# New order lists for a three-engine attention and gated-MLP kernel, with LayerNorm statistics on VectorE in some blocks and the last output transfers moved

## The chip, the cores and the metric

One NeuronCore of one Trainium2 chip runs the whole kernel. The metric is device time in microseconds (us), the median of several executions. One further execution was recorded by the hardware profiler, and the durations below come from it.

Engine names in the profile: PE is TensorE (PEld its weight loads), DVE is VectorE, ACT is ScalarE, POOL is GpSimd, SP is SyncE, which here issues nearly all DMA transfers. A trailing q (SPq) marks the sequencer of an engine.

## The reference

Eight batches, eight heads, 576 positions, head dimension 64. Attention keeps only the scores within `tau` of the row's maximum; a gated MLP with a spatial projection follows.

```python
scores = scale * q @ k^T                                # 64 problems of 576 x 576
scores = where(scores >= max(scores) - tau, scores, -1e9)
attn   = exp(scores - max) ; attn /= sum(attn)
x      = (attn @ v), heads side by side                 # [8, 576, 512]
h      = relu(x @ w_in) ; u, v = h[:512], h[512:]
v_n    = (v - mean(v)) / sqrt(var(v) + 1e-6)            # over the 512 features
v_s    = w_spatial @ v_n + b_spatial                    # over the 576 positions
out    = (u * v_s) @ w_out
```

## The kernel before

**Pairs and steps.** Heads are worked in pairs, four pairs to a batch. A pair has four row blocks of 128 positions; the last 64 positions of two pairs share one block more. So a batch has 18 steps, and step `g` is one block of 128 rows by 2 heads by 576 columns of scores. The scores lie in a ring of two PSUM tiles (`s_ring`), so step g+2 can begin on TensorE only when step g's scores have been read.

**A step in tokens.** `S` computes most of the scores on TensorE (line 678), `G` is an empty instruction on POOL that waits for the first of them, `Y` computes the rest behind `G` (they share a bank), `M` takes the negated maxima on VectorE (line 708). Then there are two ways:
- on the ScalarE path (`on_act`, listed in `ON_ACT`), `B` turns the maxima into biases (line 714), `E` and `F` apply a Prelu with a huge negative slope to the two heads (line 723), so that scores under the threshold become hugely negative, and `Z` takes the exponentials of both heads at once (line 743);
- on the VectorE path, `E` and `F` are exponentials (line 726), and `W` masks them with one VectorE instruction (line 738).

Two blocks of numerators are then turned by a DMA transpose on SyncE: `T` (`turn_p`, line 749), and `TR` for the shared block (line 755). Some of these are done on TensorE instead (`RP`).

**Around the steps.** `QA`/`QB`/`QR` transpose q and k on TensorE, and `qa`/`qb`/`qr` evict them; `kd` and `sq`/`sv` are POOL's copies. `P` and `p` multiply with v and divide (lines 376 to 390), likewise `R`/`r`. `XP`/`xp` and `X` transpose the result x, on TensorE or by DMA. The MLP of the batch before runs between the steps: `v` (lines 514 to 529), `u` (576), `s` (605) and `o` (634) are matmul groups, and `ev`, `eu`, `es`, `eo` their evictions. `L` issues loads, `C..` prepares the weights (`Ci` is w_in, `Cs` the spatial matrix, `Co` w_out, `Cb` the bias), `OUT1` and `OUT3` send two finished output blocks each (line 653), and `OUT4` the last 64 rows (line 566). A leading `d` puts an eviction on VectorE instead of ScalarE.

**LayerNorm in a block.** The evictions of `v` take five instructions over three engines: `ev` is a Relu on ScalarE with the row sums (line 537, followed by a read of the accumulator), `n` makes the negated mean on POOL (line 545), `k` squares on ScalarE with a sum (line 551, again with a read), and `N` makes the reciprocal root and the normalised block with four POOL instructions (lines 557 to 561).

**The order.** The order is written out. `ORDER` holds four lists of tokens; batch 0 runs the first, batch 1 the second, batch 2 the third, and batches 3 to 7 all run the fourth. A token `s1:2` means "for the batch two before this one", `L1:-1` "for the next". Each engine works its own instructions in the order in which the tokens issue them, and semaphores do the rest; nothing is reordered at run time. After the lists come the two tokens of `LAST` (the last mask and the last transpose), and then a tail without lists: the rest of batch 6's MLP and the whole of batch 7's, whose LayerNorm uses `bn_stats` and `bn_aggr` on VectorE (lines 784 and 786).

Of the kernel before, what the change touches and what calls it, by code (L numbers as in the profile page):

```python
# [16 lines left out]
    "L1:-1 L7:0 S0:0 G0:0 Y0:0 L0:-1 S1:0 M0:0 G1:0 Y1:0 QA1:0 L8:0 M1:0 E0:0 QR1:0 F0:0 B1:0 qa1:0 W0:0 "  # L17
    "S2:0 E1:0 G2:0 Y2:0 F1:0 dqr1:0 M2:0 Z1:0 S3:0 G3:0 kd1:0 Y3:0 E2:0 T00:0 QB1:0 M3:0 F2:0 qb1:0 B3:0 "
    "W2:0 F3:0 S4:0 E3:0 G4:0 Y4:0 Z3:0 M4:0 S5:0 Ci1:0 G5:0 Y5:0 sq2:0 L4:-1 QR2:0 B4:0 M5:0 Ci2:0 F4:0 "
    "QB2:0 E4:0 Cb0:0 dqb2:0 Z4:0 S6:0 T01:0 dqr2:0 B5:0 G6:0 sv0:0 Y6:0 F5:0 RP01:0 M6:0 QA2:0 E5:0 "  # L20
    "rp01:0 B6:0 qa2:0 QR3:0 E6:0 S7:0 G7:0 F6:0 Y7:0 M7:0 Z5:0 Ci0:0 S8:0 G8:0 kd2:0 L9:0 Y8:0 sq3:0 "
    "Z6:0 B7:0 M8:0 sv1:0 qr3:0 QB3:0 E7:0 RP00:0 B8:0 F7:0 kd3:0 T10:0 Cis1:0 drp00:0 E8:0 S9:0 F8:0 "
    "G9:0 Y9:0 Z8:0 M9:0 S10:0 G10:0 sq0:-1 Y10:0 Z7:0 B9:0 dqb3:0 Cis0:0 Cs1:0 M10:0 F9:0 QA3:0 L6:-1 "
    "R0:0 E9:0 dqa3:0 S11:0 B10:0 r0:0 G11:0 Cbs0:0 F10:0 Y11:0 P00:0 E10:0 M11:0 T11:0 sv2:0 Z9:0 S12:0 "
    "G12:0 sv3:0 B11:0 Y12:0 F11:0 P10:0 M12:0 Cis2:0 E11:0 Z11:0 Ci3:0 p00:0 L3:-1 p10:0 P01:0 Z10:0 "
    "Cs2:0 S13:0 p01:0 G13:0 sq1:-1 B12:0 Y13:0 F12:0 M13:0 T20:0 P11:0 E12:0 Css2:0 XP0:0 p11:0 dxp0:0 "
    "XP1:0 B13:0 E13:0 dxp1:0 QA0:-1 S14:0 F13:0 L2:-1 G14:0 Cis3:0 qa0:-1 Y14:0 L5:-1 QR0:-1 M14:0 "
    "QB0:-1 qr0:-1 Css4:0 XR0:0 Z12:0 S15:0 dqb0:-1 G15:0 F14:0 kd0:-1 Y15:0 P20:0 M15:0 E14:0 T21:0 "
    "Z13:0 S16:0 G16:0 B15:0 Css3:0 p20:0 Y16:0 E15:0 M16:0 F15:0 L7:-1 S17:0 W14:0 F16:0 G17:0 L8:-1 "
    "Y17:0 Z15:0 M17:0 E16:0 W16:0 T30:0 P21:0 F17:0 E17:0 p21:0 L9:-1 Cs0:0 "),  # L30
(
    "RP11:1 S0:0 G0:0 Y0:0 drp11:1 WS2:1 M0:0 RP10:1 ws2:1 S1:0 rp10:1 G1:0 Y1:0 B0:0 E0:0 QR1:0 M1:0 "
    "QA1:0 qr1:0 F0:0 qa1:0 B1:0 S2:0 W17:1 E1:0 G2:0 sq2:0 Y2:0 F1:0 QB1:0 M2:0 T31:1 Z0:0 XP2:1 S3:0 "
    "G3:0 sv1:0 qb1:0 dxp2:1 Y3:0 F2:0 M3:0 P30:1 kd1:0 E2:0 QB2:0 Z1:0 S4:0 B3:0 p30:1 G4:0 Y4:0 Co0:1 "
    "E3:0 QA2:0 M4:0 Css0:1 L5:-1 F3:0 qa2:0 S5:0 dqb2:0 Z3:0 G5:0 Y5:0 B4:0 W2:0 QR2:0 T00:0 P31:1 qr2:0 "
    "E4:0 R1:1 p31:1 F4:0 M5:0 XP3:1 S6:0 xp3:1 G6:0 kd2:0 Y6:0 r1:1 E5:0 L1:-1 M6:0 F5:0 WS0:1 L4:-1 "
    "v0:1 Z4:0 B6:0 S7:0 dws0:1 ev0:1 W5:0 G7:0 sq3:0 Y7:0 F6:0 T01:0 v1:1 E6:0 M7:0 RP00:0 ev1:1 S8:0 "
    "Z6:0 G8:0 n0:1 drp00:0 Cos0:1 Y8:0 QB3:0 M8:0 sv0:0 E7:0 L0:-1 v2:1 qb3:0 Css1:1 XR1:1 F7:0 QA3:0 "
    "E8:0 W7:0 S9:0 n1:1 ev2:1 G9:0 Y9:0 F8:0 T10:0 v3:1 dqa3:0 sv3:0 M9:0 S10:0 ev3:1 G10:0 k0:1 Y10:0 "
    "B9:0 P01:0 M10:0 E9:0 N0:1 u3:1 Co1:1 F9:0 B10:0 L3:-1 p01:0 S11:0 eu3:1 L6:-1 W8:0 G11:0 E10:0 "  # L40
    "Y11:0 F10:0 QR3:0 v4:1 dqr3:0 M11:0 Z10:0 T11:0 u1:1 ev4:1 S12:0 deu1:1 F11:0 G12:0 kd3:0 Y12:0 "
    "sq0:-1 Z9:0 RP01:0 P00:0 drp01:0 n2:1 L8:-1 M12:0 n3:1 u0:1 E11:0 n4:1 Cos1:1 k2:1 S13:0 B12:0 eu0:1 "
    "p00:0 G13:0 N2:1 Y13:0 F12:0 QB0:-1 M13:0 k1:1 T20:0 P11:0 qb0:-1 sq1:-1 p11:0 E12:0 WS4:1 B13:0 "
    "R0:0 dws4:1 Z12:0 sv2:0 QR0:-1 r0:0 S14:0 E13:0 L2:-1 G14:0 dqr0:-1 N1:1 W11:0 Y14:0 F13:0 QA0:-1 "
    "k4:1 WS3:1 M14:0 S15:0 k3:1 qa0:-1 G15:0 Y15:0 T21:0 B14:0 dws3:1 WS1:1 N3:1 F14:0 dws1:1 u4:1 E14:0 "
    "M15:0 P20:0 Z13:0 S16:0 B15:0 G16:0 eu4:1 p20:0 kd0:-1 Y16:0 N4:1 E15:0 Co2:1 XP0:0 M16:0 P10:0 "
    "F15:0 L7:-1 Z15:0 TR1:0 S17:0 dxp0:0 G17:0 p10:0 Y17:0 E16:0 M17:0 P21:0 F16:0 s0:1 Z14:0 p21:0 "
    "W16:0 u2:1 E17:0 T30:0 Cos2:1 eu2:1 es0:1 F17:0 Co3:1 XR0:0 L9:-1 "),
(
    "S0:0 G0:0 Y0:0 XP2:1 M0:0 QR1:0 S1:0 qr1:0 xp2:1 G1:0 kd1:0 Y1:0 sq2:0 B0:0 E0:0 QB1:0 M1:0 QA1:0 "  # L50
    "F0:0 qb1:0 S2:0 B1:0 W17:1 E1:0 G2:0 Y2:0 qa1:0 s1:2 F1:0 M2:0 T31:1 Z0:0 XP1:1 S3:0 B2:0 es1:2 G3:0 "
    "F2:0 sv0:0 Y3:0 dxp1:1 s2:2 E2:0 M3:0 sq3:0 Z1:0 QB2:0 L0:-1 B3:0 es2:2 S4:0 F3:0 L7:-1 G4:0 E3:0 "
    "Y4:0 L5:-1 P30:1 M4:0 qb2:0 Z2:0 S5:0 G5:0 p30:1 T00:0 Y5:0 B4:0 QR2:0 M5:0 s3:2 E4:0 qr2:0 F4:0 "
    "QA2:0 es3:2 F5:0 S6:0 dqa2:0 Z4:0 G6:0 Cos3:2 Y6:0 sv1:0 P31:1 M6:0 E5:0 R1:1 kd2:0 Z3:0 TR0:0 p31:1 "
    "S7:0 G7:0 r1:1 sv2:0 Y7:0 F6:0 o0:2 M7:0 X1:1 E6:0 o1:2 eo0:2 W6:0 T01:0 F7:0 o2:2 E7:0 W5:0 S8:0 "
    "eo1:2 G8:0 eo2:2 Y8:0 o3:2 M8:0 L4:-1 v0:1 eo3:2 L1:-1 B8:0 W7:0 E8:0 S9:0 ev0:1 G9:0 Y9:0 F8:0 u2:1 "
    "M9:0 T10:0 Z8:0 QR3:0 S10:0 deu2:1 G10:0 n0:1 F9:0 sv3:0 Y10:0 dqr3:0 v1:1 M10:0 E9:0 QA3:0 ev1:1 "
    "OUT3:2 W9:0 S11:0 qa3:0 G11:0 sq0:-1 E10:0 Y11:0 v2:1 M11:0 F10:0 k0:1 s4:2 kd3:0 W10:0 ev2:1 T11:0 "
    "S12:0 G12:0 F11:0 n2:1 Y12:0 es4:2 E11:0 QB3:0 M12:0 v3:1 qb3:0 u1:1 W11:0 ev3:1 L9:-1 F12:0 n3:1 "
    "S13:0 L3:-1 E12:0 G13:0 N0:1 Y13:0 eu1:1 u3:1 M13:0 k2:1 P00:0 k3:1 T20:0 B13:0 S14:0 p00:0 eu3:1 "  # L60
    "G14:0 N3:1 W12:0 F13:0 Y14:0 v4:1 E13:0 M14:0 R0:0 ev4:1 L2:-1 S15:0 r0:0 F14:0 G15:0 OUT4:2 n1:1 "
    "N2:1 Y15:0 k1:1 QB0:-1 M15:0 OUT1:2 P01:0 qb0:-1 E14:0 p01:0 T21:0 P20:0 N1:1 B15:0 P10:0 E15:0 "
    "p20:0 F15:0 S16:0 p10:0 G16:0 n4:1 W14:0 Y16:0 k4:1 QR0:-1 u4:1 qr0:-1 kd0:-1 QA0:-1 M16:0 eu4:1 "
    "N4:1 u0:1 qa0:-1 L8:-1 Z13:0 P11:0 B16:0 L6:-1 deu0:1 S17:0 p11:0 F16:0 G17:0 sq1:-1 Y17:0 Z15:0 "
    "s0:1 M17:0 E16:0 T30:0 P21:0 es0:1 F17:0 p21:0 E17:0 Z16:0 TR1:0 X0:0 "),
(
    "S0:0 G0:0 Y0:0 QA1:0 M0:0 QR1:0 qa1:0 S1:0 qr1:0 G1:0 B0:0 Y1:0 W17:1 E0:0 QB1:0 F0:0 s1:2 M1:0 "
    "qb1:0 Z0:0 S2:0 T31:1 G2:0 es1:2 Y2:0 B1:0 s3:2 M2:0 F1:0 E1:0 R1:1 sv1:0 es3:2 S3:0 B2:0 r1:1 F2:0 "
    "L3:-1 G3:0 kd1:0 Y3:0 sq2:0 E2:0 L1:-1 s2:2 M3:0 Z1:0 sq3:0 S4:0 B3:0 es2:2 F3:0 G4:0 Y4:0 T00:0 "
    "E3:0 o0:2 M4:0 Z2:0 P30:1 deo0:2 S5:0 B4:0 p30:1 G5:0 E4:0 Y5:0 F4:0 QA2:0 M5:0 L0:-1 P31:1 Z3:0 "  # L70
    "S6:0 p31:1 qa2:0 G6:0 sv2:0 Y6:0 X1:1 F5:0 o1:2 M6:0 sv3:0 E5:0 o2:2 eo1:2 W5:0 T01:0 E6:0 QB2:0 "
    "F6:0 S7:0 eo2:2 G7:0 W6:0 Y7:0 qb2:0 S8:0 Z4:0 G8:0 sv0:0 Y8:0 M7:0 L7:-1 QR2:0 s4:2 qr2:0 L4:-1 "
    "kd2:0 v0:1 es4:2 E7:0 M8:0 v1:1 F7:0 ev0:1 W7:0 S9:0 T10:0 ev1:1 G9:0 Y9:0 F8:0 n1:1 QR3:0 o3:2 "
    "dqr3:0 M9:0 E8:0 v2:1 k1:1 W8:0 eo3:2 S10:0 L6:-1 ev2:1 G10:0 n0:1 TR0:0 Y10:0 E9:0 P01:0 n2:1 M10:0 "
    "kd3:0 sq0:-1 F9:0 P00:0 k0:1 S11:0 B10:0 p01:0 F10:0 T11:0 G11:0 N0:1 p00:0 Y11:0 E10:0 QB3:0 M11:0 "
    "v3:1 qb3:0 Z10:0 W9:0 QA3:0 S12:0 OUT3:2 ev3:1 G12:0 dqa3:0 Y12:0 E11:0 OUT1:2 v4:1 M12:0 F11:0 u1:1 "
    "ev4:1 W11:0 T20:0 S13:0 eu1:1 n4:1 G13:0 Y13:0 B12:0 N1:1 E12:0 QR0:-1 M13:0 R0:0 qr0:-1 F12:0 "
    "QA0:-1 k2:1 S14:0 B13:0 r0:0 G14:0 F13:0 N2:1 Y14:0 dqa0:-1 E13:0 P10:0 L8:-1 M14:0 Z12:0 P11:0 "
    "OUT4:2 n3:1 L2:-1 S15:0 p10:0 k4:1 G15:0 kd0:-1 p11:0 Y15:0 F14:0 N4:1 u4:1 M15:0 T21:0 P20:0 eu4:1 "
    "E14:0 u0:1 p20:0 k3:1 B15:0 W14:0 u2:1 F15:0 E15:0 S16:0 deu0:1 Z13:0 G16:0 N3:1 Y16:0 deu2:1 u3:1 "  # L80
    "M16:0 Z15:0 X0:0 QB0:-1 sq1:-1 S17:0 eu3:1 B16:0 dqb0:-1 G17:0 E16:0 TR1:0 Y17:0 s0:1 F16:0 M17:0 "
    "Z16:0 T30:0 P21:0 es0:1 E17:0 p21:0 F17:0 L5:-1 L9:-1 ")]
LAST = "W17:1 T31:1"
ON_ACT = [(1, 3, 4, 5, 6, 7, 8, 9, 10, 11, 12, 13, 15), (0, 1, 3, 4, 6, 9, 10, 12, 13, 14, 15), (0, 1, 2, 3, 4, 8, 13, 15, 16), (0, 1, 2, 3, 4, 10, 12, 13, 15, 16)]


@with_exitstack
def kernel(
    ctx: ExitStack,
    tc: tile.TileContext,  # L90
    q: bass.AP,
    k: bass.AP,
# [427 lines left out]
    def moe_v(b, c):  # L520
# [13 lines left out]
        def ev():  # L534
# [4 lines left out]
            if c == 4 and b:  # L539
                o = hold["o"] = orr.tile([P, 512], F32, name="o")  # L540
                nc.scalar.copy(out=o[64:128], in_=hold["t"][64:128])
# [503 lines left out]
```

## Time and profile before

| what | us |
|---|---|
| median of 8 executions | 446.6 |
| lowest, highest | 445.94, 447.68 |
| the profiled execution's own time | 446.49 |
| its span, first to last instruction | 444.6 |
| busy: PE, DVE, ACT, POOL | 413.5, 394.0, 388.1, 181.4 |

The granted TensorE clock was 0.998 over the span. The span is the time from the first instruction to the last; 1.9 us of that execution's own time lie outside it. A row of a group gives the line, engine, operation, tiles and shapes, the count, then the busy time and the mean of one in ns, and then the idle time of the engine just before these instructions with what ended it. A row of the chain of waits gives start, length and what ran or was waited for. A row of the busy time by stretch gives the stretch, its length, the busy time and number of instructions of each engine, the clock, the DMA share and GB/s.

Two instructions of one engine can overlap by about a tenth of a microsecond, so the mean duration is longer than what one instruction adds to its engine's queue. TensorE's busy time includes matmuls in flight and says less about how much room it has.

### The profile page before, as it was taken

What the parts mean: (1) busy time and instruction counts of PE and PEld (TensorE: products, weight loads), DVE (VectorE), ACT (ScalarE), POOL (GpSimd) and SP (SyncE); (2) the same over time, 40 slices, a digit from 0 to 9 for tenths busy, and PEclk for the clock granted to TensorE, in tenths of its full rate; (3) what the DMA queues carried; (4) which work ended last, traced back from release to release, by engine and by line L of the source; (5) the groups of instructions that cost most, each with busy time, mean ns of one, the idle gap of its engine ahead of it and who ended that gap; (6) DMA issues with size and microseconds to landing.
All of it is one profiled execution on the core that took longest, in us unless ns stands there. A gap on an engine that the chain in (4) does not pass through costs nothing.

```text
span 444.6 us, 12872 instructions
## 1 busy us (share of the span) xinstructions
PE 413.5 (93%) x5035; PEld 259.6 (58%) x5035; DVE 394.0 (89%) x615; ACT 388.1 (87%) x649; POOL 181.4 (41%) x403
## 2 busy tenths in 40 slices
PE   7776789989999899999999999999999999999995
PEld 4445565565656666665565666566665666566542
DVE  5878889899899889999999999999999999999673
ACT  3997999999989899999899998999899998999351
POOL 1255334573215724354343533455343523354031
PEclk9999999999999999999999999999999999999999
DMA  7999999799999999999999999999999997998713
GB/s 189 283 260 201 247 229 193 138 213 205 215 174 243 193 199 198 191 229 218 200 206 203 251 174 206 238 206 234 192 215 196 250 188 148 162 210 122 169 35 108
DMA packets 222556, 88.15 MB, mean 198 GB/s; under 512 B 193568, under 2 KB 218272, under 8 KB 222496
## 3 DMA queue, kind: packets, MB, share of 16 engines
q1 hardware_dynamic: 221840, 86.45, 95.2%
q8 instruction: 40, 0.66, 0.6%
q0 software_dynamic: 160, 0.52, 0.3%
q10 hardware_dynamic: 496, 0.36, 0.2%
q14 instruction: 20, 0.16, 0.1%
HBM read 32.79 MB, written 9.44 MB: 95 GB/s over the span
## 4 chain that ended last, share of the span: by engine, by line
PE 32%; DVE 24%; ACT 18%; issue 7%; DMA 4%; POOL 2%; DVEq 0%; POOLq 0%; SPq 0%; ACTq 0%
PE s L678 13%; DVE p L738 7%; ACT e L726 7%; DVE s L708 6%; DVE negm L708 5%; PE f L605 4%; ACT e L723 4%; PE f L576 3%; PE f L329 3%; PE f L381 2%; ACT p L743 2%; DVE xn L390 2%; DMA ptr<-pr 2%; ACT vrel L537 2%; ACT sq L551 1%
## 5 line engine op out<-in xcount | busy, mean ns | idle before, releaser
L678 PE MATMUL s<-qkT 64*64 64x160 f32 (+1 forms) x2304 | 172.3, 415 | 11.0 <-ACT e L723 6.4
L678 PEld LDWEIGHTS s<-qkT 64*64 64x64 f32 x2304 | 106.7, 131 | 66.2 <-ACT e L723 15.7
L723 ACT ACTIVATE e<-s,negm 128x576 f32<-128x576 f32 x166 | 115.1, 743 | 14.7 <-DVE negm L714 6.3
L708 DVE TENSOR_REDUCE s<-s 128x2 f32<-128x1152 f32 x83 | 113.1, 1362 | 13.0 <-PE s L678 10.6
L726 ACT ACTIVATE e<-s,negm 128x576 f32<-128x576 f32 x122 | 85.6, 753 | 7.7 <-DVE negm L708 7.3
L708 DVE TENSOR_REDUCE negm<-s 128x2 f32<-128x1152 f32 x61 | 82.4, 1351 | 8.8 <-PE s L678 6.8
L738 DVE SCALAR_TENSOR_TENSOR p<-e,ctau 128x1152 bf16<-128x1152 f32 x61 | 86.3, 1417 | 3.3 <-ACT e L726 3.2
L743 ACT ACTIVATE p<-e 128x1152 bf16<-128x1152 f32 x67 | 78.2, 1172 | 0.4
L215 POOL CAST v<-vl 128x512 bf16<-128x512 f32 x32 | 21.0, 658 | 72.6 <-PE s L678 68.4
L381 PE MATMUL f<-v,pT 128*128 128x65 bf16 x1008 | 44.6, 194 | 0.0
L381 PEld LDWEIGHTS <-pT 128*128 128x128 bf16 x1024 | 41.5, 98 | 2.3 <-issue 0.4
L545 POOL TENSOR_SCALAR nmean<-sm 128x1 f32<-128x1 f32 (+1 forms) x35 | 15.8, 458 | 55.0 <-PE s L678 34.5
L390 DVE TENSOR_TENSOR xn<-f,r 128x256 bf16<-128x256 f32 (+1 forms) x93 | 35.4, 381 | 2.9
L605 PE MATMUL f<-wsT,vn 128*128 128x512 bf16 x135 | 33.6, 380 | 0.0
L576 PE MATMUL f<-xT,w_in 128*128 128x512 bf16 x120 | 30.8, 380 | 0.8 <-DVE negm L714 0.4
L376 PE MATMUL f<-v,pT 128*128 128x130 bf16 x126 | 27.8, 220 | 2.3 <-DVE r L388 1.5
L192 POOL COPY qn<-ql 128x512 f32<-128x512 f32 x31 | 20.1, 647 | 21.1 <-PE s L678 20.2
L561 POOL TENSOR_SCALAR vn<-vrel,rs,nm 128x512 bf16<-128x512 f32 (+1 forms) x35 | 26.8, 767 | 3.8
L529 PE MATMUL f<-w_in,xT 128*128 128x512 bf16 x112 | 27.9, 379 | 0.2 <-ACT vrel L537 0.2
L551 ACT ACTIVATE sq<-vrel,nmean 128x512 bf16<-128x512 f32 (+1 forms) x35 | 25.8, 736 | 1.7 <-POOL nmean L545 1.5
L634 PE MATMUL f<-w_o,gT 128*128 128x512 bf16 x100 | 24.6, 379 | 1.2 <-ACT qkT L309 1.2
L341 POOL COPY qkT<-qkT 64x64 f32<-64x64 f32 x32 | 7.5, 235 | 39.8 <-PE s L678 19.8
(159 smaller groups left out, 588.4 us busy)
## 6 DMA issues: line engine op xcount, KB each, us to landing
vl<-in_v_dram SPq DMA_DIRECT2D x16, 512.0 KB, 5.1
kl<-in_k_dram SPq DMA_DIRECT2D x15, 512.0 KB, 4.9
ql<-in_q_dram SPq DMA_DIRECT2D x15, 512.0 KB, 4.8
out_dram<-oo SPq DMA_DIRECT2D x12, 512.0 KB, 4.2
uT<-in_moe_w_in_dram SPq DMA_DIRECT2D x3, 512.0 KB, 5.1
uT<-in_moe_w_spatial_dram SPq DMA_DIRECT2D x2, 576.0 KB, 5.3
vx<-in_v_dram SPq DMA_DIRECT2D x16, 64.0 KB, 3.5
pT<-p SPq DMA_TRANSPOSE x64, 6.1
```

The source lines that it names most:

```text
L381: nc.tensor.matmul(out=t[:, at + 65 * h:at + 65 * h + 65], lhsT=pt[:, 5 * h + j, :], rhs=vt[:, 6 * h + j, :], start=False, stop=(h == 1 an ...
L390: nc.vector.tensor_tensor(out=dst, in0=o[ps, g0:g1, 0:64], in1=r[ps, g0:g1].unsqueeze(2).broadcast_to([ps.stop - ps.start, g1 - g0, 64]), ...
L529: nc.tensor.matmul(out=t, lhsT=x_of(b, f, slice(c * P, (c + 1) * P)), rhs=w_in[:, f, 512:1024], start=(f == 0), stop=(f == 3))
L551: nc.scalar.activation(out=sq[:n], in_=hold["vrel"][:n], func=ACT.Square, bias=hold["nmean"][:n], accum_out=ss[:n])
L576: nc.tensor.matmul(out=t, lhsT=w_in[:, m, f * P:(f + 1) * P], rhs=x_of(b, m, slice(0, 512)), start=(m == 0), stop=(m == 3))
L605: nc.tensor.matmul(out=t, lhsT=vn[:, c, f * P:(f + 1) * P], rhs=wsT[:, c, 0:512], start=(c == 0), stop=(c == 4))
L678: made.append(nc.tensor.matmul(out=s_ring[g % 2][halves[k], at[h] + lo:at[h] + hi], lhsT=qks[n][halves[h], 0, m:m + 64], rhs=qks[n][halves ...
L708: nc.vector.tensor_reduce(out=nm, in_=view(s_ring[g % 2], at[0], [[at[1] - at[0], 2], [1, S]]), axis=AX.X, op=ALU.max, negate=True)
L723: nc.scalar.activation(out=e, in_=s, func=ACT.Prelu, bias=bias_, scale=scale if steps[g][1] == 4 else 1.0, alpha=1e30)
L726: nc.scalar.activation(out=e, in_=s, func=ACT.Exp, bias=bias_)
L738: nc.vector.scalar_tensor_tensor(out=numerators(g), in0=ef, scalar=ctau, in1=ef, op0=ALU.is_ge, op1=ALU.mult)
L743: nc.scalar.activation(out=numerators(g), in_=e_ring[g % 3].rearrange("p h s -> p (h s)"), func=ACT.Exp)
```

## The change

1. All four lists are written anew. The order of scores, maxima, exponentials, evictions, loads and MLP groups differs throughout; the fourth list stays closest to what it was.
2. In some blocks the LayerNorm statistics go to VectorE: token `bv` is the Relu without sums, `bs` is `bn_stats` and `bn_aggr`, and `n` and `k` fall away. `N` keeps its four POOL instructions.
3. `ON_ACT` changes in the first three lists: from 13, 11, 9 and 10 steps to 11, 11, 12 and 10.
4. `M` can be split into one maximum for each head, tokens `H` and `K` (steps 4 and 17 of the second list, step 11 of the third).
5. `OUT` tokens of the last batch (7) are held and run after `LAST`, that is, behind the last transposed transfer on SyncE. In the fourth list `OUT1` and `OUT3` also move from the middle to the end.

```diff
-ON_ACT = [(1, 3, 4, 5, 6, 7, 8, 9, 10, 11, 12, 13, 15), (0, 1, 3, 4, 6, 9, 10, 12, 13, 14, 15), (0, 1, 2, 3, 4, 8, 13, 15, 16), (0, 1, 2, 3, 4, 10, 12, 13, 15, 16)]
+ON_ACT = [(1, 3, 4, 5, 7, 8, 10, 11, 12, 13, 15), (0, 2, 3, 4, 6, 9, 11, 12, 13, 15, 16), (0, 1, 3, 4, 5, 6, 9, 11, 12, 13, 14, 16), (0, 1, 2, 3, 4, 10, 12, 13, 15, 16)]
...
-        def ev():
+        def ev(sums=True):
             vrel = hold["vrel"] = vr.tile([P, 512], F32, name="vrel")
-            sm = hold["sm"] = small.tile([P, 1], F32, name="sm")
-            nc.scalar.activation(out=vrel[:n], in_=hold["t"][:n], func=ACT.Relu,
-                                 accum_out=sm[:n])
+            if sums:
+                sm = hold["sm"] = small.tile([P, 1], F32, name="sm")
+                nc.scalar.activation(out=vrel[:n], in_=hold["t"][:n], func=ACT.Relu,
+                                     accum_out=sm[:n])
+            else:
+                nc.scalar.activation(out=vrel[:n], in_=hold["t"][:n], func=ACT.Relu)
...
+        def stats():
+            st = small.tile([P, 6], F32, name="st")
+            mv = hold["mv"] = small.tile([P, 2], F32, name="mv")
+            nc.vector.bn_stats(out=st[:n], in_=hold["vrel"][:n])
+            nc.vector.bn_aggr(out=mv[:n], in_=st[:n])
...
-            nc.gpsimd.tensor_scalar(out=rs[:n], in0=hold["ss"][:n], scalar1=1.0 / 512,
-                                    scalar2=1e-6, op0=ALU.mult, op1=ALU.add)
+            if "mv" in hold:
+                nc.gpsimd.tensor_scalar(out=rs[:n], in0=hold["mv"][:n, 1:2], scalar1=1.0,
+                                        scalar2=1e-6, op0=ALU.mult, op1=ALU.add)
+            else:
+                nc.gpsimd.tensor_scalar(out=rs[:n], in0=hold["ss"][:n], scalar1=1.0 / 512,
+                                        scalar2=1e-6, op0=ALU.mult, op1=ALU.add)
...
-    def top(g):
+    def top(g, heads=slice(0, 2)):
...
+        elif kind == "OUT" and it == B - 1 and (name, b) not in held:
+            held.append((name, b))
+            return
...
         for tok in LAST.split():
             run_token(tok, B)
+        for name, b in held:
+            run_token(name, b)
```

The end of the fourth list, before and after:

```diff
-    "OUT4:2 n3:1 L2:-1 S15:0 p10:0 k4:1 G15:0 kd0:-1 p11:0 Y15:0 F14:0 N4:1 u4:1 M15:0 T21:0 P20:0 eu4:1 "
-    "E14:0 u0:1 p20:0 k3:1 B15:0 W14:0 u2:1 F15:0 E15:0 S16:0 deu0:1 Z13:0 G16:0 N3:1 Y16:0 deu2:1 u3:1 "
-    "M16:0 Z15:0 X0:0 QB0:-1 sq1:-1 S17:0 eu3:1 B16:0 dqb0:-1 G17:0 E16:0 TR1:0 Y17:0 s0:1 F16:0 M17:0 "
-    "Z16:0 T30:0 P21:0 es0:1 E17:0 p21:0 F17:0 L5:-1 L9:-1 ")]
+    "S14:0 qa0:-1 G14:0 B13:0 N2:1 bs4:1 Y14:0 F13:0 P10:0 L9:-1 M14:0 E13:0 P11:0 L2:-1 Z12:0 OUT4:2 "
+    "S15:0 p10:0 G15:0 N4:1 E14:0 Y15:0 p11:0 u4:1 M15:0 T21:0 P20:0 eu4:1 F14:0 u0:1 B15:0 k3:1 p20:0 "
+    "S16:0 deu0:1 E15:0 G16:0 N3:1 Y16:0 F15:0 u2:1 M16:0 Z13:0 u3:1 deu2:1 kd0:-1 Z15:0 TR1:0 sq1:-1 "
+    "S17:0 B16:0 deu3:1 G17:0 E16:0 Y17:0 W14:0 F16:0 QB0:-1 X0:0 s0:1 qb0:-1 M17:0 Z16:0 P21:0 T30:0 "
+    "es0:1 F17:0 p21:0 E17:0 OUT1:2 OUT3:2 ")]
```

Blocks whose statistics move, by list: none in the first; blocks 0, 2, 3, 4 in the second; all five in the third; blocks 1 and 4 in the fourth. Evictions marked `d` in each list: 9, 14, 5, 7 before and 4, 11, 4, 6 after.

## The prediction

> **What bounds the kernel now.** I first read the page's busy shares and the engine shares of the chain that ended last.
>
> ```profile
> PE 413.5 (93%) x5035; PEld 259.6 (58%) x5035; DVE 394.0 (89%) x615; ACT 388.1 (87%) x649; POOL 181.4 (41%) x403
> ...
> PE 32%; DVE 24%; ACT 18%; issue 7%; DMA 4%; POOL 2%; DVEq 0%; POOLq 0%; SPq 0%; ACTq 0%
> ```
>
> No engine owns the time: three are near 90% and the chain changes hands among them. So the second view is busy time by stretch. I cut where each batch's first score matmul starts (rows two to nine are batches 0 to 7; before them is the start-up, after them the tail).
>
> ```profile
> core 0: us, PE busy (x) PEld busy (x) DVE busy (x) ACT busy (x) POOL busy (x), PEclk, DMA share, GB/s
> 0.00:7.40 7.40, 5.08 (x23) 3.71 (x23) 3.43 (x20) 2.97 (x5) 0.92 (x7) 1.00 0.68 181
> 7.40:54.00 46.60, 34.31 (x475) 23.09 (x475) 37.13 (x57) 39.48 (x54) 20.60 (x44) 1.00 1.08 241
> 54.00:106.20 52.20, 47.19 (x612) 30.75 (x612) 47.78 (x75) 49.07 (x82) 26.68 (x56) 1.00 0.97 202
> 106.20:159.30 53.10, 50.88 (x629) 32.32 (x628) 48.10 (x68) 47.73 (x84) 23.02 (x50) 1.00 1.00 204
> 159.30:210.20 50.90, 50.06 (x622) 31.33 (x620) 48.01 (x71) 48.56 (x83) 20.59 (x49) 1.00 1.07 207
> ...
> 311.20:361.60 50.40, 49.91 (x623) 31.41 (x620) 47.70 (x71) 47.44 (x82) 21.81 (x49) 1.00 1.03 212
> 361.60:409.50 47.90, 46.88 (x586) 29.14 (x584) 44.91 (x67) 44.98 (x79) 19.30 (x44) 1.00 0.86 158
> 409.50:444.60 35.10, 29.50 (x261) 15.15 (x257) 21.80 (x51) 13.59 (x23) 4.70 (x6) 0.97 0.42 110
> ```
>
> The reader is to see that batches 3 to 6, which all run the fourth list, take 50.3 to 50.9 us with VectorE idle for only 2.7 to 3.2 us. Batches 1 and 2 take 52.2 and 53.1 with VectorE idle 4.4 and 5.0. Batch 0 has 9.5 idle. There is room in the first three lists and little in the fourth. The clock is full, so the clock explains nothing.
>
> Third, the groups with their shapes apart give the price of what the change touches.
>
> ```profile
> L551 ACT ACTIVATE sq<-vrel,nmean 128x512 bf16<-128x512 f32 x28 | 20.7, 740 | 0.1
> L537 ACT ACTIVATION_READ_ACCUMULATOR vrel<-f 128x1 f32 x28 | 6.2, 221 | 0.0
> L551 ACT ACTIVATION_READ_ACCUMULATOR sq<-vrel,nmean 128x1 f32 x28 | 6.1, 217 | 0.0
> L545 POOL TENSOR_SCALAR nmean<-sm 128x1 f32<-128x1 f32 x28 | 8.4, 309 | 37.8 <-PE s L678 34.5 <-ACT vrel L537 3.4
> L784 DVE BATCH_NORM_STATS2 st<-vrel 128x6 f32<-128x512 f32 x4 | 2.7, 686 | 0.7 <-ACT vrel L782 0.7
> L786 DVE BATCH_NORM_AGGREGATE mv<-st 128x2 f32<-128x6 f32 x4 | 0.7, 182 | 0.1
> ```
>
> The last batch already takes its statistics on VectorE (L784, L786), so the added operation has a row. Last, the SyncE queue and the chain at the end of batch 7:
>
> ```profile
> 398.50 0.55 SPq L566 DMA_DIRECT2D out_dram<-o  x1
> ...
> 409.50 7.92 SPq L749 DMA_TRANSPOSE pT<-p  x2
> 417.58 0.47 SPq L649 DMA_DIRECT2D out_dram<-ql  x1
> ...
> 411.98 1.27 ACT e L726 x2
> 413.27 1.42 DVE p L738
> 414.69 1.81 DVE gT L619 x3
> 416.54 0.39 PE t L634
> ```
>
> Batch 7 ends on ScalarE (an almost unbroken run of its instructions from 398 us), then one mask and three gates on VectorE, and only then the output products.
>
> **Statistics.** A block whose token becomes `bv`/`bs` loses the square, two accumulator reads and POOL's mean. What ScalarE gets back is start to start, not the sum of durations, since neighbours overlap: in the timeline a square starts at 399.38 and the instruction behind its read at 400.09 (0.71); the Relu's read costs 0.10 (read 394.64, next start 394.74). That is 0.81 per block. VectorE pays the pair: statistics start at 423.12, the instruction behind the aggregate at 424.06, so 0.94, more than 686+182 ns because the aggregate waits for its own input. Counting tokens: none in batch 0, 4 blocks in batch 1, 5 in batch 2, 2 in each of 3 to 7: 19 blocks.
>
> **Steps moved between engines.** A step on the ScalarE path costs ScalarE 1172+2x743 ns and VectorE 1366+155; on the other path 2x753 and 1351+1417. Moving one costs VectorE 1.25 us or gives it back. `ON_ACT` has 13, 11, 9, 10 steps before and 11, 11, 12, 10 after.
>
> **Evictions.** A `d` token puts an eviction on VectorE (0.68 for 512 columns of f32, 0.29 for 128, 0.41 for `xp`, about 0.45 for `rp`). The tokens go from 9, 14, 5, 7 to 4, 11, 4, 6.
>
> **VectorE by batch.** 0: two more masks, +2.5, against evictions -2.5: zero. 1: statistics +3.7, evictions -1.0, split maxima +0.2: +2.9. 2: statistics +4.7, three masks fewer -3.75, evictions -0.4, one split maximum +0.1: +0.6. 3 to 6: statistics +1.9, `qa0` and `qb0` back to ScalarE -1.4, `eu3` +0.7: +1.2 each. 7: the same without `qa0` and `qb0`, which it never had: +2.5. Sum +10.8. ScalarE gets about 2.4, 0.2, 0.9 (four times) and 2.2 back in batches 1 to 7: 8.4. TensorE's work is unchanged; POOL loses 19 means of 0.3 to 1.0 us.
>
> **Where I weigh a rule.** VectorE is busy 47.7 of 50.4 us in a fourth-list batch, ScalarE 47.4. The Trainium skill (Perfetto Trace Analysis, Identifying the Most-Contended Engine) says that for these two engines occupancy is a fair measure of the limit and that the most occupied one is to be relieved first; this change loads it. Carried one to one to the end, +10.8 makes 457.4. But the rows show batch 2 at 53.1 us and batch 5 at 50.3 with VectorE busy 48.1 and 47.6: order is worth more here than half a microsecond of occupancy. I take the rows: new length = VectorE's new busy time + the idle time that is left.
>
> **The idle time left.** In a fourth-list batch the 2.7 idle us contain 1.4 of waiting for scores and 0.5 for other named waits. The scores are late because ScalarE frees the score bank late (weight loads wait 1.0 and 0.6 us on its two forms of `e`). ScalarE now has 0.9 us less to do, so I take 1.0 off: 1.7. Between no relief (2.7) and no wait at all (about 0.8) that is my choice, and the ends go into the range.
> - Batches 3 to 6: 48.8+1.7 = 50.5 against 50.9, 50.7, 50.3, 50.4: -0.3 in all.
> - Batch 1: 50.7+1.7 = 52.4: +0.2.
> - Batch 2: 48.7+2.3 = 51.0: -2.1. More idle time is left since TensorE is busy 50.9 there.
> - Batch 0: equal load, 9.5 idle. 3.4 of it is one ramp wait that stays; two reorderable waits of 1.5 (the `xp` evictions at 43.6 to 46 us) should halve: -0.8.
> - Batch 7: 47.4+1.7 = 49.1 by VectorE, but its end hangs on ScalarE, which loses 2.2. I take zero; bounds -1.3 and +1.2.
>
> **Waits that move.** POOL's normalisation waited for ScalarE's square and now waits for VectorE's aggregate; behind it in POOL's queue stand the `G` turns that let TensorE write the second half of a score bank, so a late aggregate would reach TensorE through POOL. In return the mean, which waited 3.4 us on the Relu in that row (and 17.1 for the 64-row blocks), is gone. I cost this at nothing: POOL has 28 of 50 us idle; with that cover gone it would be the 0.3 us by which one score wait typically lasts. The split maximum (`H`/`K`, three times) has no row; from 680 ns for 512 columns and 424 for 256 one half of 576 is 0.74, so a pair costs 0.12 more and can let a head start 0.6 earlier: -0.6 to +0.12, taken as +0.1 in the sums. Loads that change places on SyncE (0.6 us to issue, 5 to land) keep a batch section of slack; cost nothing, or up to 1 us once if one becomes late.
>
> **Outputs.** `OUT1` and `OUT3` go to the end of each fourth-list batch, past `T11`, `T20`, `T21`, `TR1` and `T30`; each issues in about 0.5 us, and the next `T31` now stands behind both, while its consumer stands some 15 us later. In batch 7 all three go behind the last transpose: 1.5 us of SyncE that ends at about 419 and delays the `ql` output of 417.58. That output is not on the chain; the last ones leave at 438 to 440. Nor did the last transpose make TensorE wait (issued 414.75, used at 418.25 behind other products). So zero; bounds -0.5 and +0.5.
>
> **Sum.** -0.8 +0.2 -2.1 -0.3 +0 = -3.0 us on a span of 444.6: 441.6. The profiled execution's own time is 446.49, so 1.9 lie outside the span, and the median of eight is 446.6, 0.1 above it. 446.6-3.0 = 443.6.
>
> **Rivals.**
> *VectorE becomes the bound.* The idle time stays at 2.7 because the waits only change names. Then batch 1 is 53.4, batch 2 51.4, batches 3 to 6 51.5, batch 7 50.1: +1.2 -1.7 +3.7 +2.2 = +5.4, with batch 0's -0.8 about +4.6: 451. It decides once more than about 2.3 us of idle time stay per batch. For it: 95% occupancy. Against: half of the present idle is waiting for scores that ScalarE holds up.
> *The lists run as meant.* Idle falls to 0.9 (1.5 in batch 2, where TensorE has more), as almost no wait is left, and batch 0 gives 1.5: -1.5, -0.6 in batch 1, -2.9 in batch 2, -3.5 for the next four, +0.4 in batch 7: about -8, 438.5. For it: the mean's hops ACT to POOL to ACT are gone. Against: TensorE is busy 49.9 of 50.4, so a fourth-list batch could hardly come below 49.7.
> *It doesn't do what it says.* TensorE is already the bound in batches 2 to 6 and gains and losses cancel: 446.6, within 0.9.
>
> **Numbers.** A difference of 0.2% (0.9 us) is about what a measurement of this kernel can tell from none. Forecast (440.5 to 445.7) 0.50, lists as meant 0.16, no change 0.12, VectorE bound 0.22. Faster 0.66, same 0.12, slower 0.22. The range takes the forecast with its open ends, most of the fast case and the milder half of the slow one: 438.5 to 449.5. The forecast's own range is 440.5 to 445.7.
>
> **What would show it.** VectorE busy near 405 us and ScalarE near 380; batch 2 near 51; fourth-list batches 50.2 to 50.8 with VectorE idle under 2; square rows down to 16, statistics rows up by 19; the tail still 35 us. Wrong if fourth-list batches exceed 51 (VectorE bound), if batch 2 stays at 53, or if the tail moves by over 1 us.

## The result and the profile after

The changed kernel takes 442.71 us (median of 11 executions), against 446.51 for the kernel before (32 executions). The ratio is 0.992, with a 95% interval of 0.9909 to 0.9931: faster by 3.8 us. The forecast was 443.6 us, with a range of 438.5 to 449.5.

First the page of the kernel after, busy shares and the chain's shares by engine:

```profile
PE 413.4 (94%) x5035; PEld 259.3 (59%) x5035; DVE 400.8 (91%) x644; ACT 380.9 (86%) x605; POOL 178.9 (41%) x384
...
PE 39%; DVE 31%; ACT 18%; issue 9%; DMA 1%; POOL 1%; POOLq 0%; DVEq 0%; ACTq 0%
```

VectorE is 6.8 us busier and ScalarE 7.2 less, TensorE as before. The span is 440.9. The chain lies on TensorE and VectorE more than it did (39 and 31%, from 32 and 24).

Busy time by stretch, kernel after, cut as before where each batch's first score matmul starts (the first row is batch 0):

```profile
8.00:52.40 44.40, 32.84 (x474) 22.93 (x474) 37.82 (x52) 39.01 (x57) 24.39 (x44) 1.00 1.03 235
52.40:103.50 51.10, 47.24 (x613) 31.23 (x612) 48.24 (x80) 47.69 (x74) 27.67 (x56) 1.00 0.97 215
103.50:155.60 52.10, 50.82 (x629) 32.48 (x625) 48.59 (x80) 48.02 (x73) 19.89 (x42) 1.00 1.03 214
155.60:206.00 50.40, 49.97 (x619) 31.11 (x616) 47.95 (x73) 46.87 (x77) 20.93 (x47) 1.00 1.03 199
...
306.90:357.40 50.50, 50.07 (x623) 31.15 (x620) 48.59 (x74) 46.56 (x77) 20.93 (x47) 1.00 1.02 209
```

The same cut to a hundredth, read from the start of each batch's first score matmul in the timelines (us), with the kernels of the experiments below, shows where the time came from:

| kernel | start + batch 0 | batch 1 | batch 2 | batch 3 | batch 6 | rest of the span |
|---|---|---|---|---|---|---|
| before | 53.96 | 52.25 | 53.06 | 50.88 | 50.36 | 83.0 |
| after | 52.38 | 51.16 | 52.05 | 50.44 | 50.44 | 83.5 |
| first3_new | 52.18 | 51.84 | 52.03 | 50.36 | 50.35 | 83.1 |
| fourth_new | 55.63 | 52.25 | 53.06 | 50.44 | 50.44 | 83.6 |
| first_list_only | 51.95 | 56.30 | 53.27 | 50.37 | 50.37 | 83.1 |
| stats_only | 54.29 | 52.25 | 53.06 | 51.79 | 51.79 | 84.5 |
| stats_back | 52.36 | 54.45 | 54.82 | 50.76 | 50.76 | 83.7 |

From before to after: start and batch 0 -1.6, batch 1 -1.1, batch 2 -1.0, batches 3 to 6 together -0.5, the rest (batch 7 and the tail) +0.5: -3.7 of the span. The fourth list, which runs five of eight batches, brought almost nothing. The -0.5 is not its doing: behind the new first three lists the old fourth list takes 50.35 to 50.36 us in each of batches 3 to 6 (first3_new). In the kernel before, the same list took 50.88 and 50.71 in batches 3 and 4 and 50.36 only later; the reason is open.

The groups of the kernel after that answer to the statistics' rows:

```profile
L560 ACT ACTIVATE sq<-vrel,nmean 128x512 bf16<-128x512 f32 x16 | 11.7, 731 | 0.0
L549 DVE BATCH_NORM_STATS2 st<-vrel 128x6 f32<-128x512 f32 x12 | 8.2, 681 | 0.1
L549 DVE BATCH_NORM_STATS2 st<-vrel 64x6 f32<-64x512 f32 x7 | 4.8, 683 | 0.2
L550 DVE BATCH_NORM_AGGREGATE mv<-st 128x2 f32<-128x6 f32 x12 | 2.2, 182 | 0.4
```

16 squares are left of 35, and 12+7 = 19 statistics are new. And the end of batch 7, first the chain of waits:

```profile
408.01 1.38 ACT e L748 x2
409.42 1.42 DVE p L760
410.83 1.81 DVE gT L637 x3
412.69 0.39 PE t L652
```

The SyncE queue of the same kernel:

```profile
406.80 6.57 SPq L771 DMA_TRANSPOSE pT<-p  x2
413.42 0.77 SPq L584 DMA_DIRECT2D out_dram<-o  x1
414.24 1.06 SPq L671 DMA_DIRECT2D out_dram<-oo  x2
```

From the start of the last mask to the end it takes 31.5 us, and took 31.3. The three outputs now follow the last two transposes.

### The profile page after: what moved, and what is told of

The parts are those of the page before. It is cut to its first block, busy times and chain, and to the rows that moved or that the text cites. A ratio compares the mean times of both kernels' runs of the same rounds, so it can differ in the third digit from the quotient of the medians.

```text
span 440.9 us, 12846 instructions
## 1 busy us (share of the span) xinstructions
PE 413.4 (94%) x5035; PEld 259.3 (59%) x5035; DVE 400.8 (91%) x644; ACT 380.9 (86%) x605; POOL 178.9 (41%) x384
## 4 chain that ended last, share of the span: by engine, by line
PE 39%; DVE 31%; ACT 18%; issue 9%; DMA 1%; POOL 1%; POOLq 0%; DVEq 0%; ACTq 0%
PE s L696 16%; DVE s L730 11%; DVE p L760 9%; ACT e L745 7%; DVE negm L730 5%; ACT e L748 4%; ACT p L765 4%; PE f L594 4%; PE f L381 3%; PE f L329 3%; DVE xn L390 2%; DVE gT L637 1%; PE f L623 1%; PE f L652 1%; PE f L529 1%
## 5 line engine op out<-in xcount | busy, mean ns | idle before, releaser
L696 PEld LDWEIGHTS s<-qkT 64*64 64x64 f32 x2304 | 106.7, 132 | 73.6 <-ACT e L745 17.5
L730 DVE TENSOR_REDUCE s<-s 128x2 f32<-128x1152 f32 (+1 forms) x86 | 114.5, 1331 | 6.7 <-PE s L696 6.3
L730 DVE TENSOR_REDUCE negm<-s 128x2 f32<-128x1152 f32 (+1 forms) x61 | 81.1, 1329 | 7.2 <-PE s L696 6.5
L192 POOL COPY qn<-ql 128x512 f32<-128x512 f32 x31 | 23.8, 767 | 71.1 <-PE s L696 70.4
L381 PE MATMUL f<-v,pT 128*128 128x65 bf16 x1008 | 44.5, 194 | 0.0
L215 POOL CAST v<-vl 128x512 bf16<-128x512 f32 x32 | 21.8, 681 | 50.6 <-PE s L696 48.5
L381 PEld LDWEIGHTS <-pT 128*128 128x128 bf16 x1024 | 41.5, 97 | 1.2
L594 PE MATMUL f<-xT,w_in 128*128 128x512 bf16 x120 | 29.6, 380 | 0.0
L311 ACT COPY qkT<-f 128x512 f32<-128x512 f32 (+1 forms) x53 | 23.7, 450 | 1.1 <-PE f L329 0.7
L329 PE MATMUL f<-identf,kn 128*128 128x128 f32 x124 | 19.9, 283 | 2.3 <-ACT xT L311 0.7
```

The lines of the kernel that those rows point to most:

```text
L329: nc.tensor.transpose(out=t[:, c * P:(c + 1) * P], in_=nat[i][which][:, c, :], identity=identf)
L381: nc.tensor.matmul(out=t[:, at + 65 * h:at + 65 * h + 65], lhsT=pt[:, 5 * h + j, :], rhs=vt[:, 6 * h + j, :], start=False, stop=(h == 1 an ...
L594: nc.tensor.matmul(out=t, lhsT=w_in[:, m, f * P:(f + 1) * P], rhs=x_of(b, m, slice(0, 512)), start=(m == 0), stop=(m == 3))
L696: made.append(nc.tensor.matmul(out=s_ring[g % 2][halves[k], at[h] + lo:at[h] + hi], lhsT=qks[n][halves[h], 0, m:m + 64], rhs=qks[n][halves ...
L730: nc.vector.tensor_reduce(out=nm[:, heads], in_=view(s_ring[g % 2], at[h0], dims), axis=AX.X, op=ALU.max, negate=True)
```

## The experiments

All ratios are to the kernel before. The first four ask which part carries the gain: the first three lists, the fourth list, or the statistics.

**Three new lists, old fourth.**

```diff
-ORDER = [new 1, new 2, new 3, new 4]
+ORDER = [new 1, new 2, new 3, old 4]        # ON_ACT likewise
```

> First three lists (and their ON_ACT) of the changed kernel, fourth list of the kernel before; outputs of batch 7 held as in the change. Theory 'warm-up lists': the traces put -1.6 us in start and batch 0, -1.1 in batch 1, -1.0 in batch 2, and only -0.2 in batches 3 to 7, so this keeps nearly all: about 443.0 (ratio 0.992 to 0.994). Rival 'statistics': the gain goes with the 19 blocks whose statistics left ScalarE; 9 of them are here, so about half: 444.7 (ratio 0.996).

Measured: 442.34 us, ratio 0.9902 (0.9885 to 0.992). The whole gain is there with the old fourth list. A batch of the old list in this kernel:

```profile
307.10:357.50 50.40, 49.53 (x617) 31.39 (x620) 47.71 (x71) 47.44 (x82) 21.81 (x49) 1.00 1.07 213
```

**Old three, new fourth.**

```diff
-ORDER = [new 1, new 2, new 3, new 4]
+ORDER = [old 1, old 2, old 3, new 4]        # ON_ACT likewise
```

> First three lists of the kernel before, fourth list of the changed kernel (10 of the 19 blocks on VectorE), outputs held. Theory 'warm-up lists': 446.0 to 446.6 (ratio 0.999 to 1.000), as batches 5 and 6 took 50.4 in both traces. Rival 'statistics': about 444.5 (ratio 0.9955).

Measured: 446.74 us, ratio 1.0007 (0.9993 to 1.002). The fourth list with its ten moved blocks is worth nothing that can be measured. Theory "warm-up lists" holds; "the gain goes with the number of blocks moved" is out.

**The new orders with the statistics back on ScalarE.**

```diff
-"... bv1:1 ... bs1:1 ..."
+"... ev1:1 ... n1:1 ... k1:1 ..."           # all 19 blocks; k where bs stood, n six tokens earlier
```

> All lists of the changed kernel, but the statistics of all 19 blocks back on ScalarE and POOL (k where bs stood, n six tokens earlier). Rival 'statistics': all of the gain is lost, 446 to 447. Theory 'warm-up lists': the order carries the gain and ScalarE has the room (46.6 busy of 50.4): 443 to 444.5, a loss of up to 1.5 us where a square now stands in ScalarE's queue.

Measured: 449.32 us, ratio 1.0062 (1.0042 to 1.0082), slower than both kernels. I had expected at most 1.5 us of loss for the order's theory, so that theory alone falls too. The busy time by stretch for batches 1 and 2, and for one batch of the fourth list:

```profile
52.40:106.80 54.40, 47.13 (x607) 31.15 (x612) 45.98 (x72) 49.97 (x86) 27.25 (x60) 1.00 0.95 206
106.80:161.60 54.80, 50.39 (x620) 32.63 (x624) 45.09 (x70) 51.62 (x88) 20.83 (x47) 1.00 0.98 203
263.20:313.90 50.70, 49.48 (x610) 31.16 (x616) 47.30 (x70) 47.63 (x83) 20.11 (x49) 1.00 1.02 213
```

In batch 2 ScalarE is now busier than VectorE (51.6 of 54.8 us), and VectorE has 9.7 us idle. Nearly all of the loss is in batches 1 and 2, which are 3.3 and 2.8 us longer than in the changed kernel; a fourth-list batch is 0.3 longer. So the second and third list count on the statistics being on VectorE; in the third list three more steps were given to ScalarE. The place of `n` and `k` was chosen by me, and another might lose less.

**The old orders with two blocks' statistics on VectorE.**

```diff
-"... ev1:1 ... n1:1 ... k1:1 ..."           # blocks 1 and 4, fourth list of the kernel before
+"... bv1:1 ... bs1:1 ..."
```

> All lists of the kernel before; only the statistics of blocks 1 and 4 in the fourth list go to VectorE (bs where k stood, n dropped). Rival 'statistics': 5 batches x 2 blocks, about 444.5 (ratio 0.9955). Theory 'warm-up lists': no measurable change, 446.0 to 447.5, and above 447.5 only if VectorE, at 47.7 + 1.9 us of 50.4, becomes the bound.

Measured: 453.46 us, ratio 1.015 (1.0135 to 1.0165). This is the prediction's slow rival, and worse. A fourth-list batch:

```profile
315.30:367.10 51.80, 49.70 (x612) 31.40 (x617) 49.15 (x75) 46.23 (x76) 21.70 (x47) 1.00 1.00 209
```

VectorE went from 47.7 to 49.15 us busy, the batch from 50.36 to 51.79. Its idle time stayed where it was (2.7 before, 2.6 now): the added work went into the time one to one. ScalarE's relief bought nothing. Another place for `bs` was not tried.

With first3_new, stats_back and the changed kernel, all four combinations of the fourth list are measured:

| fourth list | statistics of blocks 1 and 4 | batch, us | VectorE idle, us |
|---|---|---|---|
| old (first3_new) | ScalarE | 50.36 | 2.7 |
| old (stats_only) | VectorE | 51.79 | 2.6 |
| new (stats_back) | ScalarE | 50.76 | 3.4 |
| new (after) | VectorE | 50.44 | 1.9 |

So in the fourth list statistics on VectorE and the new order are not two gains that add: each alone is a loss, and together they come back to where the old list stood. For the second and third list the statistics without the new order were not run, nor were their order, `ON_ACT`, evictions and split maxima taken apart. Which of these carries the gain of batches 1 and 2 is open, beyond that it is lost without the statistics on VectorE.

**Where the first list's gain goes by itself.**

```diff
-ORDER = [new 1, new 2, new 3, new 4]
+ORDER = [new 1, old 2, old 3, old 4]        # ON_ACT likewise
```

> Only the first list and its ON_ACT of the changed kernel, no statistics on VectorE at all; the rest as before, outputs held. If batch 0's gain is its own and carried to the end: batch 1 starts near 52.2 instead of 54.0 to 55.6, the later batches keep 52.2, 53.1 and 50.4 to 50.9, and the time is 444.3 to 445.0 (ratio 0.995 to 0.997). If it is taken up by the next lists, which were fitted to the old first list: 446 to 447.

Measured: 446.34 us, ratio 0.9994 (0.9981 to 1.0007). Batch 1 does start 2.0 us earlier (51.95), but then takes 56.30 instead of 52.25. The profiled execution was one of the slow ones, 447.92 us against that median, so it shows the seam at its worst. The SyncE queue:

```profile
58.30 0.58 SPq L168 DMA_DIRECT2D vl<-in_v_dram  x1
58.98 0.45 SPq L256 DMA_DIRECT2D uT<-in_moe_w_spatial_dram  x1
59.54 5.05 SPq L771 DMA_TRANSPOSE pT<-p  x1
```

The chain of waits (start, length, what):

```profile
59.54 8.43 DMA pT<-p
```

TensorE's waits from 52 to 108 us (total, times, longest):

```profile
PE f L376 <- DMA pT<-p: 2.7, 2, 2.5
```

TensorE's busy time by stretch (the figure behind the count is the granted clock):

```profile
65.50:68.00 2.50, 0.01 (x1) 0.75 0.95 249
68.00:73.60 5.60, 5.58 (x62) 0.50 0.96 207
```

The same place in the SyncE queue of the kernel before:

```profile
58.19 0.44 SPq L256 DMA_DIRECT2D uT<-in_moe_w_spatial_dram  x1
60.94 3.03 SPq L749 DMA_TRANSPOSE pT<-p  x1
```

A transpose whose issue starts 0.1 us after that of two large loads (512 and 576 KB) has ended lands 8.4 us later; TensorE waits 2.5 us for it, and then works at half its clock for 5.6 us. In the kernel before, the transpose after the same two loads was issued 2.3 us after the second one's issue had ended; it landed after 6.35 us, at 67.29, and its product began at 67.56. In the kernel after it is issued 0.1 us behind them and lands as late (8.46 us, at 67.19), but the new second list has other work on TensorE up to then, and its product begins at 67.23. A list's gain holds only if the next list's consumers fit the times at which it hands over.

The halved clock makes the loss larger and is not the whole of it: of the fourteen executions, the three with a mean clock of 0.999 or 1.00 took 445.09, 445.62 and 446.10 us. That is about 1 us better than the kernel before (446.65 in the same session), where the earlier start of batch 1 was worth 2.0.

**Without holding the outputs.**

```diff
-elif kind == "OUT" and it == B - 1 and (name, b) not in held:
+elif kind == "OUT" and False and (name, b) not in held:
```

> The changed kernel without holding the outputs of batch 7 (they go where the fourth list has them: the last 64 rows before the last transposes, the two pairs between T30 and T31). Prediction's reading: no change within 0.5 us, since TensorE waits for no transpose there. Rival: T31 stands 1 us later behind the two pairs and shares the DMA engines with 1 MB of output, and the P product waits: +1 to +3 us.

Measured: 447.86 us, ratio 1.0032 (1.002 to 1.0045), 5 us slower than the changed kernel. The SyncE queue of that kernel:

```profile
409.36 1.07 SPq L671 DMA_DIRECT2D out_dram<-oo  x2
410.53 4.55 SPq L771 DMA_TRANSPOSE pT<-p  x1
```

Its chain of waits:

```profile
410.53 7.88 DMA pT<-p
418.41 0.05 issue
418.46 0.29 PE f L376
418.75 0.44 PE f L381 x8
```

TensorE's waits from 405 to 425 us:

```profile
PE f L376 <- DMA pT<-p: 2.8, 1, 2.8
```

And its busy time by stretch with the clock:

```profile
414.00:418.40 4.40, 1.66 (x23) 1.00 0.96 244
418.40:421.80 3.40, 2.81 (x26) 0.50 0.16 61
```

In the changed kernel the product that needs the last transpose stands here:

```profile
415.87 0.22 PE L376 MATMUL f<-v,pT 128*128 128x130 bf16 x1
```

It is the same mechanism. Behind two outputs of 512 KB the last transpose lands after 7.88 us instead of 4.88; the product that needs it starts 9.4 us after the start of the last mask instead of 6.5 (415.87 less 409.42); and the clock is halved for 3.4 us behind the wait. The eight small products of `L381` take 0.44 us instead of 0.25. The spans differ by 3.7 us: the product comes 3.0 us later after the mask, what follows it takes 1.1 longer, and the mask stood 0.4 earlier. The profiled execution is the fastest of the six (446.40 us); what makes the difference of the medians larger, 5.1 us, has no trace. The mean clock was 0.990 to 0.995 in all six, and 0.998 or more in ten of the twelve executions of the changed kernel, so the fall of the clock is no accident of one execution.

Whether the transpose is held up because it queues behind the copies or because it shares the DMA engines with them was not tested. Nor is it late each time: in the changed kernel, transposes issued within 0.3 us behind a copy landed after 4.7 to 8.5 us.

**The hold alone, in the old orders.**

```diff
+# lists of the kernel before; outputs of batch 7 run after LAST
```

> All lists of the kernel before; only the outputs of batch 7 are held until behind the last transpose. Theory 'the hold repairs what the fourth list's new place for the outputs would cost': here they stood early (392 and 398 us), so nothing: 446.0 to 447.0. Rival 'the hold is worth 4 us by itself': 442 to 443.

Measured: 446.57 us, ratio 1.0001 (0.9993 to 1.0009). There the outputs had long been sent, at 392 and 398 us. So the hold is no gain in itself: it repairs what the fourth list's new place for `OUT1` and `OUT3` would cost in the last batch.

**What sets a fourth-list batch: three doses.**

```diff
+st0 = small.tile([P, 6], F32, name="st0")                      # dve_more: once more, b >= 2
+nc.vector.bn_stats(out=st0[:n], in_=hold["vrel"][:n])
...
+nc.scalar.activation(out=sq[:n], in_=vrel[:n], func=ACT.Square)   # act_more: in bv, b >= 2
...
+nc.tensor.matmul(out=t, lhsT=vn[:, 0, f * P:(f + 1) * P],         # pe_more: before the group, b >= 2
+                 rhs=wsT[:, 0, 0:512], start=True, stop=True)
```

> The changed kernel with each moved statistics instruction issued once more, unused, in the batches of the fourth list: 2 x 0.68 us of VectorE per batch. If VectorE sets the fourth list's 50.44 us: 51.5 to 51.8 a batch and about 449 in all. If TensorE sets it: 50.4 to 50.8, 443 to 444.5. If the order of waits among all three sets it, something between.

> The changed kernel with an unused square behind the Relu of the two moved blocks in the fourth list: 2 x 0.61 us of ScalarE per batch, what the moved statistics took off it. If ScalarE's room is real (46.6 busy of 50.44): 50.4 to 50.6 a batch, 442.5 to 443.5. If ScalarE is in a chain with VectorE: up to 51.6, 448.

> The changed kernel with the first product of each of the four wide spatial groups issued twice in the batches of the fourth list: 4 x 0.216 us = 0.86 us of TensorE per batch. If TensorE sets the 50.44 us: 51.2 to 51.3 a batch, about 447. If VectorE sets it: 50.4 to 50.7, 442.7 to 444.

Measured: 450.44, 444.36 and 448.11 us, ratios 1.0111 (1.0075 to 1.0147), 0.9954 (0.994 to 0.9968) and 1.0041 (1.0025 to 1.0057). A late batch of dve_more in the busy time by stretch:

```profile
259.60:311.60 52.00, 50.02 (x621) 31.12 (x620) 50.10 (x76) 46.62 (x77) 21.05 (x47) 1.00 0.97 206
```

Of act_more:

```profile
308.50:359.30 50.80, 50.15 (x620) 31.13 (x617) 48.79 (x74) 47.44 (x79) 20.49 (x47) 1.00 1.05 211
```

Of pe_more:

```profile
308.80:360.00 51.20, 50.86 (x625) 31.49 (x621) 48.93 (x75) 46.69 (x76) 20.93 (x47) 1.00 1.01 209
```

From 50.44 us, 1.36 us more on VectorE gives 51.99 (+1.55, VectorE idle still 1.9), 0.86 on TensorE gives 51.15 (+0.71), 1.22 on ScalarE 50.80 (+0.35). In busy time of a batch the doses came to 1.56, 0.80 and 0.94 us. VectorE binds fully, TensorE almost, and ScalarE in part: none of the three single answers that I had set against each other is the right one.

**Taking work off VectorE.**

```diff
-"... deu3:1 ..."
+"... eu3:1 ..."          # eu3_act; eu2_eu3_act has deu2:1 -> eu2:1 too
```

> The changed kernel with one eviction of the fourth list (u3) back on ScalarE: VectorE loses 0.60 us of queue time per batch, ScalarE gains 0.49. From the doses (1.55 us longer for 1.36 us on VectorE, 0.35 for 1.22 on ScalarE): if the slope of VectorE also holds downwards, -0.6 +0.14 = about -0.45 a batch, 50.0, and 440.4 in all. If TensorE is the next bound right below (its slope was 0.71 for 0.86), 50.3 to 50.44 and 442 to 442.7.

> The same with u2 as well: VectorE loses 1.2 us a batch, ScalarE gains 0.98. VectorE's slope alone would give 49.5 a batch and 438.5; if TensorE or ScalarE takes over as the bound, no better than with one eviction, 50.2 to 50.8 a batch.

Measured: 443.54 us, ratio 0.9936 (0.9923 to 0.995), and 447.36 us, ratio 1.0016 (1.0008 to 1.0024). The batches got longer, 50.6 to 50.7 and 51.1 to 51.5. VectorE's slope does not hold downwards. That the relief is spent by the eviction that now stands in ScalarE's queue is my reading, and no run here shows it. Neither of the two moves tried gained; other tokens were not tried.

No kernel here is shown to beat the changed one: first3_new's 442.34 and the changed kernel's 442.71 have overlapping intervals.

## Why the prediction was right, point by point

- **VectorE's added load, forecast +10.8 us; ScalarE's, -8.4.** Measured +6.8 and -7.2 busy. The term that was mis-sized is VectorE's: the pair of statistics was priced at 0.94 us from the last batch, where the instruction behind the aggregate waits for the aggregate. In the lists an independent instruction follows and starts 0.10 us after it, so in 17 of 19 cases the pair takes 0.82 (0.72+0.10); that is 2.3 us over 19 blocks. And I added up durations of evictions and masks, which overlap their neighbours when they stand close: one by one, the durations on VectorE grew by 10.1 us in the trace, and its busy time, which counts an overlap once, by 6.8.
- **A fourth-list batch, forecast 50.5.** Measured 50.44. VectorE's idle time in it, forecast 1.7, is 1.9. Added work on VectorE in stats_only and dve_more left the idle time as it was, so "new busy time plus idle left" described what VectorE's load does. That the idle time fell from 2.7 because scores come earlier with a lighter ScalarE was my argument, and it is not what the runs show: stats_only has the lighter ScalarE and keeps 2.6. The new order alone does not bring it either: stats_back has 3.4. It takes both, so the 1.7 came out near by a reason that does not hold by itself, and that is luck in part.
- **Batch 1, forecast +0.2, and batch 2, -2.1.** Measured -1.1 and -1.0. The sum, -1.9 forecast and -2.1 measured, is right, the parts are not: they are off by 1.3 and 1.1 in opposite directions, and that they cancel is luck. Batch 1's VectorE load was over-sized by the term above (48.2 us busy, not 50.7). Batch 2 keeps 3.5 us of VectorE idle time, where I had left 2.3; TensorE is busy 50.8 us in it.
- **Batch 0, forecast -0.8.** Measured -1.6 with the start. The direction was right, the size was half. The sum also took for granted that a gain in batch 0 lasts. It did with the new second list; with the old one nothing of it was left in the median, and about half in the few executions at full clock.
- **Batch 7 and the tail, forecast 0.** Measured +0.5 of the span, inside the bounds given.
- **The outputs, forecast zero.** Right as a sum of two edits, 31.3 us against 31.5 from the last mask to the end, but the working was wrong. I set the last transpose against the product at 418.25, which reads the one before. It landed at 419.44 and its own product began at 419.73: there was 0.3 us of room. Moving `OUT1` and `OUT3` without the hold costs 3.7 us by the spans and 5.1 by the medians, and the hold gives it back; the bounds of half a microsecond held by that alone.
- **The weighed rule** (the Trainium skill, Perfetto Trace Analysis, Identifying the Most-Contended Engine: relieve the most occupied engine first). The sum by the rule was 457.4. Taking the rows was right for this change, whose lists were written for its loads. With orders left as they were, the rule was right: stats_only went to 453.46. Nor does the new order make VectorE's load free: dve_more paid 1.55 us a batch for 1.36.

## What to carry to other kernels

In a hand-written order whose batches keep three engines busy for over 90% of the time, moving work and ordering it are one edit. In the fourth list here the moved statistics alone cost 1.4 us a batch and the new order alone 0.4, and both together next to nothing; taking the statistics out of all the new lists turned a gain of 3.8 us into a loss of 2.8. Cut such a trace by batch and by list, and look at the seams: a list that ends earlier helps only if the next one's consumers fit. Before calling a transfer hidden, write down when it lands and when its own consumer starts; the last transpose landed 3 us later here when it was issued right behind two large copies.

## What the runs showed of the hardware that I had not expected

- A short wait can cost twice. TensorE waits of 2.5 us (first_list_only, 65.5 to 68.0) and 2.8 us (no_hold, 415.7 to 418.5) went with a granted clock of 0.50 from 66.8 to 73.6 us and from 418.4 to 421.8 us. In no_hold, what followed the wait took 1.1 us longer. The Trainium skill (TensorE: Matmul & The Clock Gate, Part 1: The HAM clock gate) names an idle window of about 3.4 us for the fall to half rate; here waits shorter than that sufficed. The length of a wait alone does not decide: all ten profiled kernels with the new first list have a wait of 1.9 us between 32 and 35 us, and only in one of them, eu2_eu3_act, was the clock halved behind it (busy time of TensorE by stretch):

```profile
35.00:38.40 3.40, 3.40 (x42) 0.50 1.03 138
```

- Many batch lengths repeat to a hundredth: batches 3 to 6 of the kernel after took 50.44, 50.44, 50.45 and 50.44 us, and batches 1 and 2 under the old lists took 52.25 and 53.06 in three different kernels. Batch 1 under the new second list is less steady, 51.16 to 51.88 in eight kernels. The start varies more: to the end of batch 0 it took 54.0 to 55.6 us with the old first list in four profiled kernels, and 51.9 to 52.6 with the new one in nine of ten. The tenth, at 53.8, is eu2_eu3_act with the halved clock above.
